# Turning x and C on TensorE, emptying PSUM in pairs, and a reordered head in a fused state-space and feed-forward kernel

## The chip, the core and the metric

The kernel runs on one core of a Trainium2 chip. A core has TensorE (PE: matrix products into PSUM, eight banks of 512 fp32 columns), VectorE (DVE), ScalarE (ACT), GpSimd (POOL) and the queue of SyncE (SP); DMAs are issued from SP, ACT or POOL. The metric is the device time of one execution in microseconds (us).

## What is computed

x is 2048 tokens by 448 features. A gate mixes a diagonal complex state-space model (448 states) with a feed-forward block (width 1792):

```python
g = sigmoid((x * gate_w).sum(-1, keepdims=True))
dt = exp(log_dt); Lam = Lambda_re + 1j * Lambda_im
Lam_bar = exp(dt * Lam)
Bu = einsum("bld,pd->blp", x, ((Lam_bar - 1) / Lam)[:, None] * Bmat)
h[t] = Lam_bar * h[t - 1] + Bu[:, t, :]          # over 2048 steps
a = 2.0 * einsum("blp,dp->bld", h, Cmat).real + x * Dskip
b = silu(x @ w1) @ w2
out = g * a + (1 - g) * b
```

All inputs and the output are bf16.

## The kernel before

**Tiling.** Tokens go in four chunks of 512 (`tc`), features and states in blocks of 128; 448 = 3 x 128 + 64. The real and imaginary parts of the 448 states fill seven slots of 128 lanes (0 to 3 real, 4 to 6 imaginary; slot 3 holds the last 64 of both). The recurrence is made real: tables COS and SIN rotate the input B x of each chunk, a real scan (`tensor_tensor_scan`, one per slot and chunk, decay `rc`) runs over it into `Gf`, and the result is rotated back into `H`.

**Stages.** `x_products` (L586 to L617) computes tiles of x times w1 (F, 14 per chunk) and of x times B (B, 7 per chunk). Two tiles run side by side, each on 64 rows of TensorE at a time; a pair takes two halves, of 4 and 3 steps, and the first half of the next pair is issued before the second of the present one. `evict` (L575) empties each tile by ScalarE: F with Silu into `aT`, B into `U`. `lanes` (L628) does the rotation, scans and back rotation of a chunk on VectorE; each scanned slot goes from fp32 `Gf` to bf16 `Gb` by a DMA of the GpSimd queue (L659). `gates` (L731) computes g. `ffn2` (L682) is the product with w2 for 128 tokens, emptied by ScalarE into `fe` and added to `xnat` by an accumulating DMA. `readout` (L701) is the product of H with the scaled C (`CP`), emptied by VectorE (L710) into `ot` and stored. `readout_weights` (L716) makes CP from C and the scales `sc1`, `nsc1`, `sc2`.

**Transposed inputs.** TensorE needs x with features on partitions. Chunk 0 is turned on TensorE (`x0_transposes`, L437); chunks 1 to 3 and both parts of C come by transposing DMAs on SP (`loadT`, L361 to L363). B is turned on TensorE (`b_transposes`, L549). The three parameter rows reach all lanes by a small product with the identity (L469); ScalarE takes their Exp; four phase tables are made on VectorE (L495 to L502) and turned into SIN and COS by ScalarE; GpSimd copies them to slots 4 to 6 (L505, L506) and computes the scales in some 25 four-column operations (L512 to L544).

**What sets the order.** Every operation is registered with an estimated cost and a priority. A list scheduler (`Plan.order`, L97) simulates the engines and writes one fixed order for each; TensorE keeps the order of the program, the others take the earliest ready operation, the lower priority number first. PSUM banks are handed out in that simulation. On the chip each engine works through its list in order and waits by semaphores.

The order of the loads on SP (L366 to L412) is: x of chunk 0, w1 columns 0 to 512 in two cuts, B, w1 columns 512 to 1792 in two cuts, x of chunk 1 transposed, gate_w and Dskip spread over the partitions (`gwb`, `dkb`), w2, then x of chunks 1 to 3 plain and of 2 and 3 transposed, then C transposed.

The order of stages on TensorE is written out at the end of the function (L750 to L785):

```python
x_products(F(0, 0, 4)); b_transposes(...)      # slots 0,1 / 2 / 4,5 / 6 / 3
x_products(B(0) + F(0, 4, 5)); lanes(0); gates(0)
x_products(F(0, 5) + B(1)); lanes(1); gates(1)
readout_weights(); ffn2(0..3)
x_products(F(1) + F(2, 0, 1) + B(2)); lanes(2); gates(2)
ffn2(4..7); readout(0..3)
x_products(F(2, 1) + B(3)); lanes(3); gates(3)
readout(4..7); ffn2(8..11)
x_products(F(3))
readout(8..11); ffn2(12..15); readout(12..15)
```

Of the kernel before, what the change touches and what calls it, by code (L numbers as in the profile page):

```python
# [32 lines left out]
class Ps:  # L33


    __slots__ = ("bank", "users", "left")

    def __init__(self):
        self.bank = None
        self.users = 0  # L40
        self.left = 0
# [7 lines left out]
class Plan:  # L49
# [4 lines left out]
    INORDER = ("pe",)  # L54

# [41 lines left out]
    def order(self):  # L97
# [8 lines left out]
        free = {}  # L106
# [5 lines left out]
        def earliest(o):  # L112
            t = 0.0
            for d in o.deps:
                p = ops[d]
                t = max(t, p.end + (self.HOP[p.eng] if p.eng != o.eng else 0.02))
            new = [x for x in o.ps_w if x.bank is None]
            if new:
                open_ = sorted(banks[b] for b in range(8) if holder[b] is None)
                if len(open_) < len(new):  # L120
                    return None
                t = max(t, open_[len(new) - 1] + 0.1)
            return t

        while len(done) < len(ops):
# [22 lines left out]
            if o.sem is not None:  # L148
                slow = o.eng == "pool"
                free[o.eng] = t + (1.0 if slow else 0.45)  # L150
                pipe[o.eng] = max(pipe.get(o.eng, 0.0), t + 0.9) + o.bytes / (100e3 if slow else 260e3)
                o.end = pipe[o.eng] + 0.7
            else:
                free[o.eng] = o.end = t + o.cost
# [4 lines left out]
            for tk in o.ps_w:  # L159
                if tk.bank is None:  # L160
                    b = min((x for x in range(8) if holder[x] is None), key=lambda x: (banks[x], x))
                    tk.bank = b
                    tk.left = tk.users
                    holder[b] = tk
            for tk in o.ps_r:
                tk.left -= 1
                banks[tk.bank] = max(banks[tk.bank], o.end)
                if tk.left == 0:
                    holder[tk.bank] = None
# [10 lines left out]
class Waits:  # L180
# [14 lines left out]
    def put(self, o):  # L195
        eng = o.eng
        reads = o.reads + [f"bank{t.bank}" for t in o.ps_r]
        writes = o.writes + [f"bank{t.bank}" for t in o.ps_w]
# [54 lines left out]
def bass_gated_mix__ssm_conv_s5__dense_activation_silu__prompt_kernel(nc, A_x, A_Lambda_re, A_Lambda_im, A_B_re, A_B_im, A_C_re, A_C_im,  # L253
               A_log_dt, A_Dskip, B_x, B_w1, B_w2, gate_w, out):
    with ExitStack() as ctx:
# [12 lines left out]
        BT = sb("BT", [128, 4, NSLOT * 128], BF16)  # L268
        CTr = sb("CTr", [128, 4, D_MOD], BF16)
        CTi = sb("CTi", [128, 4, D_MOD], BF16)  # L270
# [7 lines left out]
        H = [sb(f"H{k}", [128, NSLOT, CH], BF16) for k in range(4)]  # L278
# [8 lines left out]
        ct = [sb(f"ct{k}", [128, D_MOD], F32) for k in range(2)]  # L287
# [11 lines left out]
        prm = sb("prm", [3, 512], BF16)  # L299
        pc = sb("pc", [128, 3, 4], F32)  # L300
# [29 lines left out]
        def bk(t):  # L330
            return ps[:, t.bank, :]
# [24 lines left out]
        def load(q, dst, src, name, nbytes, prio=None, after=()):  # L356
            nl[0] += 1
            prio = nl[0] if prio is None else prio
            P.add(q, lambda e: e.dma_start(dst, src), list(after), name.split(), 0.3, prio, sem(), nbytes, tag="ld " + name)  # L359

        def loadT(dst, src, name, nbytes, after=()):  # L361
            nl[0] += 1
            P.add("sp", lambda e: e.dma_start_transpose(dst, src), list(after), [name], 0.3, nl[0], sem(), nbytes, tag="ldT " + name)  # L363


        for k, v in enumerate((A_Lambda_re, A_Lambda_im, A_log_dt)):  # L366
            load("act", prm[k:k + 1, 64:512], v.rearrange("(o n) -> o n", o=1), f"prm{k}", 896, k)
# [3 lines left out]

        def load_w1(c0, c1, name):
            load("sp", w1s[:, 0:3, c0:c1], B_w1[0:384, c0:c1].rearrange("(b p) f -> p b f", p=128), name + "a", 768 * (c1 - c0))
            load("sp", w1s[:, 3, c0:c1], B_w1[320:448, c0:c1], name + "b", 256 * (c1 - c0))

        w1cuts = [0, 256, 512, 1152, 1792]
        load_w1(0, 256, "w1_0")
        load_w1(256, 512, "w1_1")
        Bnat = H[3][:, :, 0:D_MOD]
        load("sp", Bnat[:, 0:3, :], A_B_re[64:448, :].rearrange("(b p) d -> p b d", p=128), "H3_0 H3_1 H3_2", 384 * 896)  # L380
        load("sp", Bnat[:, 4:7, :], A_B_im[64:448, :].rearrange("(b p) d -> p b d", p=128), "H3_4 H3_5 H3_6", 384 * 896)
        load("sp", Bnat[0:64, 3, :], A_B_re[0:64, :], "H3_3", 64 * 896)
        load("sp", Bnat[64:128, 3, :], A_B_im[0:64, :], "H3_3i", 64 * 896)
        btn = {s: [f"BT{s}"] for s in range(7)}
        load_w1(512, 1152, "w1_2")
        load_w1(1152, 1792, "w1_3")

        def load_xT(tc):
            for c, n in ((0, 3), (3, 1)):
                loadT(xT[:, c:c + n, tc * CH:(tc + 1) * CH],  # L390
                      x2[tc * CH:(tc + 1) * CH, XCOL[c]:XCOL[c] + 128 * n], f"xT{tc}{c}", CH * 256 * n)

        def load_xn(tc):
# [3 lines left out]
        load_xT(1)  # L397
        load("sp", gwb[:, :],
             gate_w.rearrange("(o n) -> o n", o=1).partition_broadcast(128).rearrange("p o n -> p (o n)"),
             "gwb", 128 * 896)  # L400
        load("sp", dkb[:, :],
             A_Dskip.rearrange("(o n) -> o n", o=1).partition_broadcast(128).rearrange("p o n -> p (o n)"),
             "dkb", 128 * 896)
# [417 lines left out]
```

## Time and profile before

| | us |
|---|---|
| median of 3 runs | 150.91 (150.79 to 153.16) |
| the profiled execution | 151.09 |
| its span, first to last instruction | 149.3 |
| TensorE busy | 137.2 |
| VectorE busy | 120.7 |
| ScalarE busy | 87.1 |
| GpSimd busy | 65.7 |

The page lists busy times, the span in 40 slices, DMA queues, the chain of waits that ended last, groups of instructions and DMA issues. A group line reads: line, engine, operation, output<-inputs, shapes, xcount | busy us, mean ns of one | idle time before them on their engine and what ended it. L603 is the product of `x_products`, L688 that of `ffn2`, L707 that of `readout`, L557 the transposes of B, L626 every two-input elementwise operation of VectorE. Matmuls are pipelined, so the mean of one is longer than their distance.

### The profile page before, as it was taken

Reading aid. Unit: us, or ns where it says so; the run is one execution under the profiler, and the core shown is the slowest. Engines: PE = TensorE matmul, PEld = TensorE weight load, DVE = VectorE, ACT = ScalarE, POOL = GpSimd, SP = SyncE. Lnnn points to the kernel's source line nnn. Section 1 sums busy time; section 2 is a strip of 40 time slices with the busy share of each in tenths; the row PEclk is TensorE's granted clock in tenths of the full one; section 3 lists DMA queues with packets and bytes.
Section 4 is the critical chain, followed back from the end, with each engine's and each line's share of the span. In section 5 each row is a group of like instructions: output and inputs, shape, how many; then the busy total and the mean of one; then the engine's idle time right before and its main releaser. Section 6 shows DMA issues by size and latency. Waiting matters only on the chain.

```text
span 149.3 us, 2605 instructions
## 1 busy us (share of the span) xinstructions
PE 137.2 (92%) x979; PEld 65.4 (44%) x979; DVE 120.7 (81%) x154; ACT 87.1 (58%) x179; POOL 65.7 (44%) x108
## 2 busy tenths in 40 slices
PE   6897925999999999999999999999999999999592
PEld 2563402344454444445554444455554445555250
DVE  0589399999199996299998999989999994946742
ACT  3579808397888498888999588720312773031100
POOL 7130796079296949245385000422750241175200
PEclk9999995699999999999999999999999999999999
DMA  4999999999999002236659100175572245547322
GB/s 135 254 296 282 60 289 317 149 258 209 212 141 164 22 0 33 31 68 102 107 79 176 39 0 0 35 141 127 93 111 31 31 75 101 129 66 101 47 56 82
DMA packets 26962, 17.35 MB, mean 116 GB/s; under 512 B 11587, under 2 KB 26822, under 8 KB 26950
## 3 DMA queue, kind: packets, MB, share of 16 engines
q1 hardware_dynamic: 19712, 10.64, 32.2%
q0 software_dynamic: 7232, 6.56, 28.8%
q8 instruction: 7, 0.11, 0.3%
q14 instruction: 5, 0.04, 0.1%
q10 hardware_dynamic: 6, 0.00, 0.0%
HBM read 6.31 MB, written 1.84 MB: 55 GB/s over the span
## 4 chain that ended last, share of the span: by engine, by line
PE 74%; SPq 8%; DVE 7%; DMA 5%; issue 2%; ACT 1%; POOL 1%; DVEq 0%; POOLq 0%
PE ps L603 38%; PE ps L688 21%; PE ps L707 14%; SPq L359 5%; SPq L363 4%; DMA gwb<-in_gate_w_dram 3%; DVE H L626 2%; DMA Gb<-Gf 2%; DVE xg L626 2%; DVE Gf L502 1%; DVE ot L710 1%; DVE PO L626 1%; DVE Gf L656 1%; ACT COS L503 0%; POOL xnat L696 0%
## 5 line engine op out<-in xcount | busy, mean ns | idle before, releaser
L603 PE MATMUL ps<-xT,w1s 64*128 64x512 bf16 x392 | 49.4, 391 | 5.0 <-ACT U L581 4.4
L688 PE MATMUL ps<-w2s,aT 128*128 128x448 bf16 x224 | 43.0, 353 | 0.0
L578 ACT ACTIVATE aT<-ps 128x512 bf16<-128x512 f32 x56 | 30.5, 598 | 15.7 <-PE ps L603 15.7
L603 PEld LDWEIGHTS ps<-xT,w1s 64*128 64x128 bf16 x392 | 20.7, 97 | 30.5 <-ACT U L581 4.9
L688 PEld LDWEIGHTS ps<-w2s,aT 128*128 128x128 bf16 x224 | 21.8, 98 | 20.9 <-issue 0.8
L359 POOL DMA_DIRECT2D Gb<-Gf x36 | 20.5, 620 | 20.9 <-DVE Gf L656 20.7
L603 PE MATMUL ps<-xT,BT 64*128 64x512 bf16 x196 | 25.3, 376 | 0.9 <-DVE BT L564 0.9
L656 DVE TENSOR_TENSOR_SCAN Gf<-rc,gin,H 128x512 f32<-128x512 f32 x21 | 25.8, 1268 | 0.1
L694 ACT ACTIVATE fe<-ps,g 128x448 bf16<-128x448 f32 x16 | 10.0, 630 | 23.9 <-PE ps L688 17.2
L707 PE MATMUL ps<-CP,H 128*128 128x448 bf16 x112 | 21.9, 353 | 1.9 <-DVE H L626 1.9
L696 POOL DMA_DIRECT2D xnat<-fe x16 | 14.9, 942 | 16.8 <-ACT fe L694 16.7
L710 DVE SCALAR_TENSOR_TENSOR ot<-ps,g,xnat 128x448 bf16<-128x448 f32 x16 | 10.9, 678 | 7.0 <-PE ps L707 6.4
L707 PEld LDWEIGHTS ps<-CP,H 128*128 128x128 bf16 x112 | 10.7, 98 | 12.8 <-DVE H L626 2.3
L581 ACT ACTIVATE U<-ps 128x512 bf16<-128x512 f32 x28 | 15.1, 599 | 2.1 <-PE ps L603 2.1
L603 PEld LDWEIGHTS ps<-xT,BT 64*128 64x128 bf16 x196 | 10.7, 94 | 12.4 <-DVE BT L564 1.1
L359 POOL DMA_DIRECT2D U<-U x8 | 4.8, 604 | 16.0 <-ACT U L581 16.0
L626 DVE TENSOR_TENSOR H<-Gb,COS 128x3584 bf16<-128x3584 bf16 x4 | 8.1, 2018 | 3.2 <-DMA Gb<-Gf 3.2
L626 DVE TENSOR_TENSOR xg<-xnat,gwb 128x1792 bf16<-128x1792 bf16 x4 | 5.9, 1477 | 5.8 <-ACT junk L740 3.3
L740 ACT ACTIVATE junk<-xg 128x448 bf16<-128x448 bf16 x16 | 9.2, 575 | 2.2 <-DVE xg L626 2.0
L747 ACT ACTIVATE xnat<-xnat,g 128x448 bf16<-128x448 bf16 x16 | 10.1, 662 | 0.1
L626 DVE TENSOR_TENSOR PI<-U,SIN 128x512 bf16<-128x512 bf16 (+2 forms) x13 | 9.0, 724 | 0.1
L626 DVE TENSOR_TENSOR H<-H,PI 128x512 bf16<-128x512 bf16 (+1 forms) x10 | 8.7, 896 | 0.1
(89 smaller groups left out, 119.7 us busy)
## 6 DMA issues: line engine op xcount, KB each, us to landing
Gb<-Gf POOLq DMA_DIRECT2D x28, 128.0 KB, 2.4
xnat<-fe POOLq DMA_DIRECT2D x16, 112.0 KB, 2.6
out_dram<-ot SPq DMA_DIRECT2D x16, 112.0 KB, 1.7
w2s<-in_B_w_dram SPq DMA_DIRECT2D x1, 1568.0 KB, 11.1
xnat<-in_A_x_dram SPq DMA_DIRECT2D x3, 448.0 KB, 5.0
w1s<-in_B_w_dram SPq DMA_DIRECT2D x2, 480.0 KB, 5.9
U<-U POOLq DMA_DIRECT2D x8, 64.0 KB, 1.9
Gb<-Gf POOLq DMA_DIRECT2D x8, 64.0 KB, 3.2
```

Of the source, the lines that this page charges most:

```text
L359: P.add(q, lambda e: e.dma_start(dst, src), list(after), name.split(), 0.3, prio, sem(), nbytes, tag="ld " + name)
L578: ACT(lambda e: e.activation(aT[tc % 2][:, k, :], bk(tk), AF.Silu), [tk, "tbl"], [f"aT{tc % 2}_{k}"], act_cost(512), 5, "silu")
L581: ACT(lambda e: e.activation(U[:, k, :], bk(tk), AF.Copy), [tk], [f"U{k}"], act_cost(512), 5, "U")
L603: r = pe.matmul(bk(tk), w[p0:p0 + 64, i, c:c + 128], xT[p0:p0 + 64, i, tc * CH:(tc + 1) * CH], start=(h == 0 and n == 0), stop=(h == 1 and ...
L626: DVE(lambda e: e.tensor_tensor(o, a, b, op), r, w, dve_cost(n, 2), prio, tag)
L656: DVE(lambda e, s=s, b=b, init=init: e.tensor_tensor_scan(Gf[:, s, :], rc[:, b:b + 1].to_broadcast([128, CH]), A[:, s, :], init, ALU.mult, ...
L688: r = pe.matmul(bk(tk)[:, 0:D_MOD], aT[tc % 2][:, fb, o:o + 128], w2s[:, fb, :], start=(fb == 0), stop=(fb == NFB - 1))
L694: ACT(lambda e: e.activation(f[:, :], bk(tk)[:, 0:D_MOD], AF.Copy, scale=g1[:, tb:tb + 1]), [tk, f"g1_{tc}"], [fn], act_cost(448, 1), 7, "fe")
L696: P.add("pool", lambda e: e.dma_start(Tb[:, tb, :], f[:, :], accum_op=ALU.add), [fn, f"Tb{tb}"], [f"Tb{tb}"], 0.3, 2, sem(), 115000, tag=" ...
L707: r = pe.matmul(bk(tk)[:, 0:D_MOD], H[tc][:, s, o:o + 128], CP[:, s, :], start=(s == 0), stop=(s == NSLOT - 1))
L710: DVE(lambda e: e.scalar_tensor_tensor(ot[tb % 3][:, :], bk(tk)[:, 0:D_MOD], g[:, tb:tb + 1], Tb[:, tb, :], ALU.mult, ALU.add), [tk, f"g_{ ...
L747: ACT(lambda e, tb=tb: e.activation(Tb[:, tb, :], xnat[:, tb, :], AF.Copy, scale=g[:, tb:tb + 1]), [f"xd{tc}", f"g_{tc}"], [f"Tb{tb}"], ac ...
```

## The change

Six edits, made together:

- No transposing DMA is left. x of chunks 1 to 3 is loaded once, plain, and turned by 16 TensorE transposes a chunk into two neighbouring PSUM banks, emptied in one operation (VectorE for chunk 1, ScalarE for 2 and 3). C is loaded plain into a part of H2's memory (in four DMAs), turned per slot into one PSUM bank and scaled straight from there; slots 3 of both parts are one.
- A pair of `x_products` takes two neighbouring banks, and where both tiles are of one kind they are emptied by one operation of 1024 columns. B of chunk 0 is emptied by VectorE.
- The loads are reordered: w1 in three cuts (0, 512, 768, 1792), gwb and dkb ahead of the last cut, x of chunk 1 and w2 behind it, then C, then x of chunks 2 and 3.
- The parameter product stands ahead of the x transposes; Exp becomes a power of e on GpSimd, so one ScalarE table load goes; five warm-up matmuls in place of seven; the last phase table has a buffer of its own; the copies of SIN and COS to slots 4 to 6 go from GpSimd to VectorE.
- The last chunk's Gb comes from ScalarE copies in place of DMAs.
- The stage order is changed, and the planner's costs for DMAs, evictions and scans, and its handing out of banks, which now knows pairs.

```diff
-        w1cuts = [0, 256, 512, 1152, 1792]
+        w1cuts = [0, 512, 768, 1792]
...
-        load_xT(1)
...
+        for dst, src, name in ((gwb, gate_w, "gwb"), (dkb, A_Dskip, "dkb")):
+            load("sp", dst[:, :], ...)
+        load_w1("sp", w1cuts[2], w1cuts[3], 0, "w1_2")
+        load_w1("sp", w1cuts[2], w1cuts[3], 1, "w1_2")
...
+        load_xn(1)
         load("sp", w2s[:, :, :], B_w2.rearrange("(fb p) d -> p fb d", p=128), "w2", F_FF * 896)
-        load_xn(1)
-        load_xT(2)
+        load_C()
         load_xn(2)
-        load_xT(3)
         load_xn(3)
-        for dst, src, name in ((CTr, A_C_re, "Cr"), (CTi, A_C_im, "Ci")):
-            loadT(dst[:, 0:3, :], src[:, 64:448], name + "a", 448 * 768)
-            loadT(dst[:, 3:4, :], src[:, 0:128], name + "b", 448 * 256)
...
-            for _ in range(7):
+            for _ in range(5):
                 r = pe.matmul(bk(tkz), zt[:, 0:128], zt, start=True, stop=True)
...
+        POOL(lambda e: e.tensor_tensor(dtc[:, :], eul[:, :], LDT, ALU.pow), ["pc", "eul"], ["dtc"], 0.35, 0)
...
+        def x_transposes(tc, who):
+            tk = Ps(2)
+            def mm(pe):
+                for q in range(4):
+                    for b in range(4):
+                        o = (q % 2 * 4 + b) * 128
+                        r = pe.transpose(bk(tk, q // 2).bitcast(BF16)[:, o:o + 128],
+                                         xnat[:, 4 * tc + b, XCOL[q]:XCOL[q] + 128], ident[:, :])
+                return r
+            PE(mm, [f"xn{tc}", "ident"], [tk], 16 * 0.056, f"xT{tc}")
...
+            if who == "dve":
+                DVE(lambda e: e.tensor_copy(dst, src()), [tk], [f"xT{tc}"], 1.25, 4, "xTe")
+            else:
+                ACT(lambda e: e.activation(dst, src(), AF.Copy), [tk], [f"xT{tc}"], act_cost(2048), 4, "xTe")
...
-        POOL(lambda e: e.tensor_copy(COS[:, 4:7, :], COS[:, 0:3, :]), ...)
-        POOL(lambda e: e.tensor_single_scalar(SIN[:, 4:7, :], SIN[:, 0:3, :], -1.0, ALU.mult), ...)
+        DVE(lambda e: e.tensor_copy(COS[:, 4:7, :], COS[:, 0:3, :]), ...)
+        DVE(lambda e: e.tensor_single_scalar(SIN[:, 4:7, :], SIN[:, 0:3, :], -1.0, ALU.mult), ...)
...
+        def evict(pair, tk):
+            kinds = [t[0] for t in pair]
+            for k, n in ((0, 2),) if kinds[0] == kinds[-1] and len(pair) == 2 else ((0, 1), (1, 1))[:len(pair)]:
...
+                if tc == 0:
+                    DVE(lambda e, src=src, dst=dst: e.tensor_copy(dst, src()), [tk], [f"U{m}" for m in names], 0.15 + 0.53 * n, 5, "U")
...
+                    if tc + 1 < NCH:
+                        load("pool", dst, src, name, 180000, 1, [f"Gf{s}"])
+                    else:
+                        ACT(lambda e, dst=dst, src=src: e.activation(dst, src, AF.Copy), [f"Gf{s}"], [name], 0.56, 6, "Gb")
...
+        def readout_weights(k):
+            tk = Ps()
...
+                        r = pe.transpose(bk16(tk)[:, o:o + 112], Cnat[:, b, c0:c0 + 128], ident[0:112, 0:112])
...
+            ACT(lambda e: e.activation(c[:, 0, :], im(), AF.Copy, scale=sc2[:, k:k + 1]), [tk, "sc2"], ...)
...
+            DVE(lambda e: e.scalar_tensor_tensor(CP[:, k, :], re(), sc1[:, k:k + 1], c[:, 0, :], ALU.mult, ALU.add), ...)
...
         x_products(F(0, 0, 4))
         b_transposes([0, 1], "dve")
-        b_transposes([2], "act")
-        b_transposes([4, 5], "dve")
-        b_transposes([6], "act")
+        b_transposes([4, 5], "act")
+        b_transposes([2], "dve")
+        b_transposes([6], "dve")
         b_transposes([3], "dve")
-        x_products(B(0) + F(0, 4, 5))
+        x_products(F(0, 4, 6) + B(0) + F(0, 6, 7))
         lanes(0)
+        x_products(F(0, 7) + B(1), {1: xt(1, "dve")})
         gates(0)
-        x_products(F(0, 5) + B(1))
         lanes(1)
         gates(1)
-        readout_weights()
-        for tb in range(0, 4):
-            ffn2(tb)
+        for f in G(0) + cp(0) + G(1) + xt(2, "act") + cp(1) + G(2) + cp(2) + G(3) + cp(3):
+            f()
         x_products(F(1) + F(2, 0, 1) + B(2))
...
-        for tb in range(4, 8):
-            ffn2(tb)
-        for tb in range(0, 4):
-            readout(tb)
+        for f in G(4) + xt(3, "act") + G(5, 6, 7) + C(0, 1, 2, 3):
+            f()
```

`G`, `C`, `cp` and `xt` stand for `ffn2`, `readout`, `readout_weights` and `x_transposes`. `{1: xt(1, "dve")}` puts chunk 1's transposes between the first half of the third pair and the second half of the second; the fourth pair's first half is the first to read them.

More of the change, by code (lines that the diff above doesn't have):

```diff
@@ L105, in order @@
                 ready.setdefault(o.eng, []).append(o)
-        free = {}
+        free = {e: 0.72 for e in ("pe", "act", "dve", "pool", "sp")}
         pipe = {}
@@ L148, in order @@
             if o.sem is not None:
[L149 to L152, printed above, removed]
+                free[o.eng] = t + o.cost
+                q = "pool" if o.eng == "pool" else "hw"
+                pipe[q] = max(pipe.get(q, 0.0), t + 0.9) + o.bytes / self.RATE[q]
+                o.end = pipe[q] + 0.8
             else:
@@ L196, in put @@
         eng = o.eng
-        reads = o.reads + [f"bank{t.bank}" for t in o.ps_r]
-        writes = o.writes + [f"bank{t.bank}" for t in o.ps_w]
+        reads = o.reads + [f"bank{t.bank + k}" for t in o.ps_r for k in range(t.n)]
+        writes = o.writes + [f"bank{t.bank + k}" for t in o.ps_w for k in range(t.n)]
         need = {}
```

292 lines of the change are left out of this document (160 added, 132 removed).

## The prediction

> **What bounds the kernel now.** I read the busy times first, then the chain of waits (its totals, then its pieces in order of time), then windows of one microsecond over the start, then the groups by form, then single engines in order of time.
>
> ```profile
> span 149.3 us, 2605 instructions
> PE 137.2 (92%) x979; PEld 65.4 (44%) x979; DVE 120.7 (81%) x154; ACT 87.1 (58%) x179; POOL 65.7 (44%) x108
> PEclk9999995699999999999999999999999999999999
> GB/s 135 254 296 282 60 289 317 149 258 209 212 141 164 22 0 33 31 68 102 107 79 176 39 0 0 35 141 127 93 111 31 31 75 101 129 66 101 47 56 82
> PE 74%; SPq 8%; DVE 7%; DMA 5%; issue 2%; ACT 1%; POOL 1%; DVEq 0%; POOLq 0%
> ```
>
> TensorE is busy 92% of the span and carries 74% of the chain, so what it does and waits for sets the time. VectorE, at 81%, stands close behind. Two slices of the clock row, from about 22 to 30 us, are at half.
>
> ```profile
> 8.26 3.94 SPq L363
> 12.25 1.34 SPq L363
> 13.63 4.66 DMA gwb<-in_gate_w_dram
> 18.41 2.65 DVE xg L626
> 21.06 1.64 DVE Gf L502
> 22.73 0.72 ACT COS L503
> 23.45 0.49 ACT U L581
> 23.99 13.79 PE ps L603 x97
> 37.78 10.70 PE ps L688 x56
> 48.48 16.73 PE ps L603 x154
> 140.96 5.48 PE ps L707 x28
> ```
>
> The columns are start, length, what. The two transposing loads of x hold SP's queue for 5.3 us (3.94 + 1.34), gwb is issued only behind them and lands at 18.3; VectorE stands in order before xg, then does the last phase table, then ScalarE its cosine, and only then the U evictions that free PSUM for TensorE at 23.99.
>
> ```profile
> 25.00:26.00 1.00, 1.00 (x8) 0.30 (x4) 1.00 (x3) 0.88 (x2) 0.02 (x1) 0.50 1.95 233
> 29.00:30.00 1.00, 1.00 (x12) 0.46 (x10) 0.87 (x4) 0.38 (x1) 0.00 (x0) 1.00 1.30 193
> L603 PE MATMUL ps<-xT,w1s 64*128 64x512 bf16 x392 | 49.4, 391 | 5.0 <-ACT U L581 4.4 <-ACT dtc L475 0.6
> L603 PE MATMUL ps<-xT,BT 64*128 64x512 bf16 x196 | 25.3, 376 | 0.9 <-DVE BT L564 0.9
> L707 PE MATMUL ps<-CP,H 128*128 128x448 bf16 x112 | 21.9, 353 | 1.9 <-DVE H L626 1.9
> ```
>
> Each window row ends in the granted clock, the DMA share and GB/s: half clock at 25, full again at 29. The groups give all of TensorE's large waits from the first product on: 4.4, 0.9 and 1.9 us. The half clock has its own price: 154 matmuls took 16.73 us later (0.1086 each), so the 97 from 23.99 should have taken 10.54 and took 13.79, a loss of 3.25. From 24 us to the end TensorE has only the last wait, so 4.4 + 3.25 + 0.9 + 1.9 = 10.45 us is all that can be won there.
>
> **The change, part by part.** First the new TensorE work.
>
> ```profile
> L557 PE MATMUL ps<-ident,H 128*128 128x128 bf16 x28 | 1.7, 219 | 0.3 <-DMA H<-in_A_B_im_dram 0.3
> 9.88 1.72 PE L557 MATMUL ps<-ident,H 128*128 128x128 bf16 x28 [0.30 <-DMA H<-in_A_B_im_dram]
> L469 PE MATMUL ps<-ident,prm 3*128 3x3 bf16 x4 | 0.2, 163 | 0.0
> L564 DVE COPY BT<-ps 128x1024 bf16<-128x1024 bf16 x2 | 1.4, 688 | 0.7 <-PE ps L557 0.7
> L564 DVE COPY BT<-ps 128x512 bf16<-128x512 bf16 x1 | 0.4, 417 | 0.0
> ```
>
> Turning x (chunks 1 to 3) takes 3 x 16 transposes, C 4 x 8: 80. At 1.72 / 28 = 0.061 us they cost 4.9 us, all on TensorE and thus on the path. The parameter product now stands ahead of the x transposes: 0.25 us.
>
> Chunk 1's transposes stand one half (3 steps of two concurrent matmuls, 6 x 0.1086 = 0.65 us) before the half that reads them, and VectorE must empty 2048 columns in between. From 1024 in 0.688 and 512 in 0.417 that copy is 1.23 us. So TensorE waits at least 1.23 - 0.65 = 0.6, and up to 0.75 more if VectorE is inside another operation; I take 1.0. The copies of chunks 2 and 3 go to ScalarE with most of an ffn2 stage (10.70 us) between, at nothing; were that cover gone they would cost at most four times the 598 ns of a 512-column row below, 2.4 us each. C's plain loads now go ahead of the last two chunks of x on SP, whose readers are two stages away: nothing.
>
> The B transposes' wait (0.9) goes: products of F blocks 4 and 5 now stand before the first B product. They need w1's second cut, the last of 2.05 MB (x 0.46, w1 0.52, B 0.80, w1 0.26); by the GB/s row, in slices of 3.73 us, that has passed by 0.50 + 0.95 MB at 7.5 us and 0.60 / 296 GB/s = 2.0 more, 9.5, and TensorE wants it when the B transposes end, now 11.6. The last cut of w1 goes behind gwb and dkb, two more issues of SP's half microsecond; TensorE wants it some six us later. Fewer warm-up matmuls and the Exp that became a power on GpSimd (no row shows it; GpSimd's four-column operations run from 0.19 to 1.99 us) lie ahead of the phase tables, behind which TensorE has transposes of B and six F blocks to do: nothing, and up to 2 us of VectorE if the power is slow.
>
> VectorE gets the U evictions of chunk 0, the chunk-1 copy and two table copies from GpSimd:
>
> ```profile
> 16.86 4.12 POOL L506 TENSOR_SCALAR SIN<-SIN 128x1536 bf16<-128x1536 bf16 x1
> L710 DVE SCALAR_TENSOR_TENSOR ot<-ps,g,xnat 128x448 bf16<-128x448 f32 x16 | 10.9, 678 | 7.0 <-PE ps L707 6.4 <-issue 0.5
> L626 DVE TENSOR_TENSOR PO<-Gb,SIN 128x1536 bf16<-128x1536 bf16 x4 | 3.8, 950 | 0.1
> L626 DVE TENSOR_TENSOR xg<-xnat,gwb 128x1792 bf16<-128x1792 bf16 x4 | 5.9, 1477 | 5.8 <-ACT junk L740 3.3 <-DMA gwb<-in_gate_w_dram 2.5
> ```
>
> By 0.678 us for 448 columns from PSUM, a pair (1024) lies between that and 1.55; I take 1.2, so 3 pairs and a single are 4.3 us. The table copies are at most 0.95 each. With 1.2 that is 7.4 us more. Against it: the wait for gwb (2.5) goes, since only those 2.05 MB are ahead of gwb; and xg, which took 2.65 beside GpSimd's 4.12 us table copy, should take the mean of the other three, (5.9 - 2.65) / 3 = 1.08, a gain of 1.6. One CP operation fewer is 0.7. VectorE thus carries some 2.6 us net more in the head, but starts its first lanes sooner and has later idle time to use:
>
> ```profile
> 40.59 1.09 DVE L626 TENSOR_TENSOR xg<-xnat,gwb 128x1792 bf16<-128x1792 bf16 x1 [3.13 <-ACT junk L740]
> 63.34 0.68 DVE L719 SCALAR_TENSOR_TENSOR CP<-CTr,sc,ct 128x448 bf16<-128x448 bf16 x1 [2.75 <-ACT ct L718]
> 129.20 2.45 DVE L656 TENSOR_TENSOR_SCAN Gf<-rc,gin,H 128x512 f32<-128x512 f32 x2
> 135.68 2.03 DVE L626 TENSOR_TENSOR H<-Gb,COS 128x3584 bf16<-128x3584 bf16 x1 [3.19 <-DMA Gb<-Gf]
> L578 ACT ACTIVATE aT<-ps 128x512 bf16<-128x512 f32 x56 | 30.5, 598 | 15.7 <-PE ps L603 15.7
> ```
>
> In the tail the last chunk's Gb goes over ScalarE (about 0.6 us a slot by the 598 ns row, on an engine then nearly idle) and no longer over DMA: the 3.19 us wait goes. Before, the last readout could start at 140.96; now at about 137.8 without any gain upstream. TensorE wants it at 139.1 (140.96 less 1.9) minus its net gain so far, 4.4 + 3.25 + 0.9 - 4.9 - 0.25 - 1.0 = 2.4, so 136.7. VectorE has to find 1.1 us in 3.13 + 2.75 of earlier idle time; I expect most, leaving 0.3. The planner's new costs reshuffle every queue, which no row prices: from 1.3 us won (both my new waits, 1.0 and 0.3, gone) to the rivals below.
>
> Emptying pairs in one ScalarE operation saves at most 0.6 us of every 1.2, but ScalarE waits 15.7 us for TensorE in this group: nothing, at the price that a bank is held some 0.5 longer, covered by three other pairs of banks.
>
> The sum: 10.45 won, less 4.9, 0.25, 1.0 and 0.3, is 4.0. Span 149.3 - 4.0 = 145.3. The profiled execution took 151.09, 1.79 beyond its span, and is 0.18 over the median, 150.91. So 147.1 us, 2.5% under the median. With no new wait at all: 145.8; and counting the last transpose's own 219 ns out of the 1.72, (1.72 - 0.22) / 27 = 0.056 each, 0.5 less: 145.3.
>
> **The rivals.** *VectorE becomes the bound.* If its 2.6 us more are not recovered and the last scan ends that much later, the last readout starts between 137.8 and 140.4; 5.48 us of TensorE and the 2.9 that follow it now (149.3 - 146.44) give spans of 146.2 to 148.8, so 148.0 to 150.6; with a slow power up to 2 more. I take 149.8. For it: 81% of the span, and 2.6 us more. Against: the 5.9 us of idle.
>
> *GpSimd's scales come late; slower.*
>
> ```profile
> 59.60 0.21 POOL L520 TENSOR_TENSOR sc<-cw 128x4 f32<-128x4 f32 x1
> 1.18 3.17 PE L431 MATMUL ps<-PO 128*128 128x512 bf16 x7 [1.18 <-DVE PO L415]
> 6.38 3.20 PE L603 MATMUL ps<-xT,w1s 64*128 64x512 bf16 x28 [0.59 <-ACT dtc L475]
> ```
>
> C now lies transposed in four PSUM banks until ScalarE and VectorE have scaled it, and that wants sc, which GpSimd finishes at 59.8 today. TensorE would start ffn2 at 37.78 - 8.55 + 0.98 + 0.25 + 1.0 = 31.5, put C there from 34, and reach the next products at 31.5 + 10.7 + 48 x 0.061 = 45. ScalarE takes its work in order, so behind a waiting scale the silus wait, banks run out two pairs later, about 48, and every microsecond beyond that is lost; with a wait of 4.4 or more the 3.25 of half clock come on top. At 53 us that is 5 + 3.25: 155. For it: today's 59.8. Against: the 4.12 us table copy and a shorter one leave GpSimd, and today nothing pressed sc to be early.
>
> *The clock comes up late.* The seven warm-up matmuls run 0.45 us apiece, twice the 0.229 of a step of the first products (3.20 / 14). With five and then a gap until the parameters land, the first 28 may run at half: up to 3.2 us more, 150.3. [...]
>
> *The transposes were not what held the loads.*
>
> ```profile
> xT<-in_A_x_dram SPq DMA_TRANSPOSE x6, 5.6
> xnat<-in_A_x_dram SPq DMA_DIRECT2D x3, 448.0 KB, 5.0
> ```
>
> A chunk of x lands in 5.6 us transposed and 5.0 plain. If bytes alone make the head late, its 4.4 and 3.25 stay: 154.8. [...] Landing times agree; the 3.94 and 1.34 us of SP's queue do not.
>
> **How the numbers follow.** Forecast 0.60 (147.1; nearly all of it over 2% faster, some 0.05 within), VectorE 0.14 (149.8), clock 0.08 (150.3), GpSimd's scales 0.15 (155), loads 0.03 (154.8). 2%, about what a measurement of this kernel can tell, is 3.0 us: below 147.9 is faster, above 153.9 slower. Faster 0.56 (0.55 and a little of the VectorE case), within 0.26, slower 0.18. The range reaches from 145.2 to 151.7, the upper parts of the VectorE and clock cases; outside lie the scales, the loads and 0.02 below.
>
> **What would show it.** Right: no TensorE wait over 2 us after the first product, a clock row without a half after the first slices, ffn2 starting near 31.5 us instead of 37.78, 128-column matmuls up by some 80 with 4.9 us or less, a wait near 1 us behind the xT copy of chunk 1. Wrong: ScalarE waiting for sc or the silus' banks holding TensorE near 48 us; a last readout that waits over 1 us for H; a half clock under the first 28 products.

## The result and the profile after

| | before | after |
|---|---|---|
| median of 4 runs, us | 150.85 (150.78 to 153.16) | 148.82 (148.56 to 149.57) |
| the profiled execution, us | 151.09 | 149.57 |
| its span, us | 149.3 | 147.6 |

The ratio is 0.987, with a 95% interval of 0.984 to 0.990: 1.3% faster, within the 2% called no change. Medians, here and below, are over all executions of a kernel; ratios and their intervals leave out executions more than 1.5% above its fastest. The profile's page after, busy times, clock row and chain totals:

```profile
span 147.6 us, 2710 instructions
PE 141.3 (96%) x1057; PEld 69.8 (47%) x1057; DVE 122.8 (83%) x160; ACT 88.2 (60%) x143; POOL 52.1 (35%) x102
PEclk9999999999999999999999999999999999999999
PE 94%; DVE 3%; issue 1%; ACT 0%; DVEq 0%
```

TensorE went from 74% of the chain to 94%, and the half slices of the clock row are gone. Most of what it waited for before is no longer there; what is left is nearly all its own work, and that has grown by 4.1 us. The chain of waits after, in order of time (start, length, what):

```profile
6.89 5.69 PE ps L642 x28
12.58 0.57 PE ps L585 x8
...
14.65 10.96 PE ps L642 x100
25.62 1.01 PE ps L508 x16
26.63 0.02 issue
26.66 1.23 DVE xT L515
27.89 0.05 issue
27.93 6.87 PE ps L642 x62
34.80 2.75 PE ps L732 x14
37.55 0.40 PE ps L768 x8
...
40.60 0.89 PE ps L508 x16
...
67.46 0.89 PE ps L508 x16
...
139.48 5.31 PE ps L751 x28
```

L642 is now the product of `x_products`, L732 that of `ffn2`, L751 that of `readout`; L508 are the transposes of x, L768 those of C (four groups of 0.40). From 14.65 on the only break is the copy L515 of chunk 1's transposes, for which TensorE waits 0.56 us. The first ffn2 starts at 34.80 instead of 37.78, 3 us earlier. Behind it come 3.4 us of transposes of x and C, and at the end the wait of 1.9 us for the last H is gone; the last product ends at 144.79 instead of 146.44, 1.65 us earlier.

The first line is what the forecast did not have: 28 matmuls in 5.69 us, where the kernel before took 3.20. Windows of one microsecond, first after, then before (the window, its length, PE's busy share and its matmuls, the other engines, and at the end the granted clock, DMA share and GB/s):

```profile
8.00:9.00 1.00, 1.00 (x7) 0.36 (x5) 1.00 (x3) 0.07 (x1) 0.87 (x2) 1.00 0.95 224
```

```profile
8.00:9.00 1.00, 1.00 (x14) 0.48 (x11) 1.00 (x3) 0.21 (x1) 0.63 (x2) 1.00 0.93 317
```

Seven matmuls against fourteen in the same microsecond, both fully busy: exactly half pace. The clock column says 1.00 in both, so it does not show this; it has to be read from the matmuls.

**The ledger.** Two terms of the forecast can now be measured better. Products of chunk 0 and B of chunk 1 between the B transposes and the first ffn2 are 168 matmuls; a later run (load order and table copies, below) does them without a break in 18.46 us. Before, they ran from 12.54 to 37.78, so 25.24 - 4.37 (the wait) - 18.46 = 2.4 us was the price of the half clock, not 3.25. The chain of before counts 97 matmuls from 23.99 on, but 64 of the 168 had run ahead of the wait, so 104 were left; the run with the table copies alone, below, shows 104 at the same place. Against the 4.0 us of the forecast, then: first matmuls -2.5, half clock -0.85, first product 0.51 later instead of 0.25, 0.4 of the wait for B's transposes still there; on the other side 80 transposes for 1.01 + 0.89 + 0.89 + 4 x 0.40 = 4.4 instead of 4.9, the wait for L515 0.56 instead of 1.0, the last readout's 0.3 not needed, and a 0.3 us wait for B's load gone. That makes 1.55, beside the 1.65 measured.

### The profile page after: what moved, and what is told of

Its sections match the earlier page's. It is cut to its first block, busy times and chain, and to the rows that moved or that the text cites. A ratio compares the mean times of both kernels' runs of the same rounds, so it can differ in the third digit from the quotient of the medians.

```text
span 147.6 us, 2710 instructions
## 1 busy us (share of the span) xinstructions
PE 141.3 (96%) x1057; PEld 69.8 (47%) x1057; DVE 122.8 (83%) x160; ACT 88.2 (60%) x143; POOL 52.1 (35%) x102
## 3 DMA queue, kind: packets, MB, share of 16 engines
HBM read 7.17 MB, written 1.84 MB: 61 GB/s over the span
## 4 chain that ended last, share of the span: by engine, by line
PE 94%; DVE 3%; issue 1%; ACT 0%; DVEq 0%
PE ps L642 45%; PE ps L732 29%; PE ps L751 15%; PE ps L508 2%; PE ps L444 2%; PE ps L484 1%; PE ps L768 1%; DVE BT L592 1%; DVE xT L515 1%; DVE ot L754 0%; ACT xT L493 0%; PE ps L585 0%; DVE PO L427 0%; PE ps L455 0%; DVE prm L457 0%
## 5 line engine op out<-in xcount | busy, mean ns | idle before, releaser
L642 PE MATMUL ps<-xT,w1s 64*128 64x512 bf16 x392 | 50.0, 391 | 1.7 <-ACT xT L493 0.8
L732 PE MATMUL ps<-w2s,aT 128*128 128x448 bf16 x224 | 43.7, 353 | 0.0
L614 ACT ACTIVATE aT<-ps 128x1024 bf16<-128x1024 f32 (+1 forms) x30 | 28.8, 964 | 17.7 <-PE ps L642 17.6
L642 PEld LDWEIGHTS ps<-xT,w1s 64*128 64x128 bf16 x392 | 20.7, 97 | 26.9 <-issue 3.8
L732 PEld LDWEIGHTS ps<-w2s,aT 128*128 128x128 bf16 x224 | 21.6, 98 | 20.2 <-issue 0.4
L642 PE MATMUL ps<-xT,BT 64*128 64x512 bf16 x196 | 25.5, 376 | 0.0
L738 ACT ACTIVATE fe<-ps,g 128x448 bf16<-128x448 f32 x16 | 10.2, 639 | 23.9 <-PE ps L732 23.3
L380 POOL DMA_DIRECT2D Gb<-Gf x27 | 16.8, 653 | 8.1 <-DVE Gf L696 8.1
L696 DVE TENSOR_TENSOR_SCAN Gf<-rc,gin,H 128x512 f32<-128x512 f32 x14 | 16.9, 1264 | 0.1
L751 PE MATMUL ps<-CP,H 128*128 128x448 bf16 x84 | 16.4, 353 | 0.0
L642 PEld LDWEIGHTS ps<-xT,BT 64*128 64x128 bf16 x196 | 10.7, 94 | 11.5
L751 PEld LDWEIGHTS ps<-CP,H 128*128 128x128 bf16 x84 | 8.1, 98 | 7.9 <-issue 0.4
L621 ACT ACTIVATE U<-ps 128x1024 bf16<-128x1024 f32 (+1 forms) x12 | 10.5, 913 | 0.9 <-PE ps L642 0.9
L380 POOL DMA_DIRECT2D U<-U x8 | 4.7, 589 | 17.7 <-ACT U L621 15.9
L666 DVE TENSOR_TENSOR PO<-Gb,SIN 128x1536 bf16<-128x1536 bf16 (+1 forms) x8 | 8.6, 1088 | 0.8 <-issue 0.5
L696 DVE TENSOR_TENSOR_SCAN Gf<-rc,gin,H2C 128x512 f32<-128x512 f32 x7 | 8.6, 1268 | 0.0
L696 DVE TENSOR_TENSOR_SCAN Gf<-rc,H 128x512 f32<-128x512 f32 x7 | 8.3, 1208 | 0.0
```

What stands on the lines that cost most here:

```text
L614: ACT(lambda e, src=src, dst=dst: e.activation(dst, src(), AF.Silu), [tk, "tbl"], [f"aT{tc % 2}_{m}" for m in names], act_cost(512 * n), 5 ...
L621: ACT(lambda e, src=src, dst=dst: e.activation(dst, src(), AF.Copy), [tk], [f"U{m}" for m in names], act_cost(512 * n), 5, "U")
L642: r = pe.matmul(bk(toks[k], b), weights(tile, p0, p0 + 64, i), xT[p0:p0 + 64, i, tc * CH:(tc + 1) * CH], start=(h == 0 and n == 0), stop=( ...
L666: DVE(lambda e: e.tensor_tensor(o, a, b, op), r, w, dve_cost(n, 2), prio, tag)
L696: DVE(lambda e, s=s, b=b, init=init: e.tensor_tensor_scan(Gf[:, s, :], rc[:, b:b + 1].to_broadcast([128, CH]), A[:, s, :], init, ALU.mult, ...
L732: r = pe.matmul(bk(tk)[:, 0:D_MOD], aT[tc % 2][:, fb, o:o + 128], w2s[:, fb, :], start=(fb == 0), stop=(fb == NFB - 1))
```

## The experiments

Each kernel ran beside the kernel before on the same chip; ratios are to that, with 95% intervals.

**Is the slow start a matter of the warm-up?** The changed kernel with seven warm-up matmuls again:

```diff
-            for _ in range(5):
+            for _ in range(7):
```

> The changed kernel with seven warm-up matmuls again instead of five, nothing else; the planner's cost for them is left, so every queue keeps its order. Theory A (the first products ran at half clock because the warm-up is shorter and a gap follows it): the first 28 matmuls take 3.2 us again instead of 5.69, the rest keeps its place behind them, and the time falls by 2 to 2.5 us, to about 146.5. Rival B (the first products were slow for another reason: they wait for w1, or the clock comes up when it likes): the 28 still take over 5 us, the time stays near 148.8.

Median 148.59 us, 0.985 (0.976 to 0.995), its runs spread from 147.75 up; the profiled one took 147.77. TensorE's matmuls in order of time there, the first 14 of the 28:

```profile
4.92 0.23 PE L455 MATMUL ps<-ident,prm 3*128 3x3 bf16 x4 [0.58 <-DVE prm L457]
5.09 1.07 PE L484 MATMUL ps<-ident,xnat 128*128 128x128 bf16 x16
7.54 1.69 PE L642 MATMUL ps<-xT,w1s 64*128 64x512 bf16 x14 [1.38 <-DVE xT L491]
```

In that execution the clock was up (28 in 3.19 us); everything in front came 0.65 us later, and ffn2 started 1.84 us earlier, at 32.96. That is the 1.8 us by which this profiled run beats the other one. But not every run followed: two took 147.8, the others 149.4 and 150.3, and no trace shows how those two began.

The reverse, five warm-ups in the kernel before:

```diff
-            for _ in range(7):
+            for _ in range(5):
```

> The kernel before with five warm-up matmuls instead of seven, nothing else. Theory A: its first 28 matmuls take 5 to 6 us instead of 3.20; but the wait of 4.4 us that follows at 19.6 us is ended by VectorE and ScalarE, not by TensorE, so most of the loss is taken back there and the time grows by under 1 us. Rival B: the 28 stay at 3.2 us. Rival C (the loss is simply added, since the head is a chain through TensorE): 2.5 us slower, 153.4.

151.56 us, 1.003 (0.998 to 1.007). The slow start is there, and its cost does not show in the times. The profile's TensorE lines

```profile
6.17 2.32 PE L603 MATMUL ps<-xT,w1s 64*128 64x512 bf16 x10 [0.54 <-ACT xT L453]
...
25.38 3.17 PE L603 MATMUL ps<-xT,w1s 64*128 64x512 bf16 x14 [4.37 <-ACT U L581]
```

show the same 4.37 us wait as before: TensorE came later to a wait that ended later too (gwb landed at 19.3 in place of 18.3). The wait ends with the U evictions behind gwb, whenever TensorE gets there. So while gwb bounded the head, a slow start could hide in that wait; the change took this cover away.

All profiled executions together, time of the first 28 products:

| warm-ups | us, one execution each |
|---|---|
| 7 | 3.20 (before), 3.19, 5.07, 3.20, 3.20, 4.92, 3.20 |
| 5 | 5.69 (after), 5.16, 4.57, 4.69, 4.87, 4.64, 5.75 |

With seven, five executions of seven start at full pace; with five, none. Seven executions of each are few, but the warm-up is all that separates the first two experiments from their kernels. (The list takes in the profiles of the runs that follow; in the one with fillers, two more matmuls stand behind the seven.)

**What held the head: the transposing DMAs, or the order of the loads?** The kernel before, its six transposing loads of x and four of C untouched, with gate_w and Dskip loaded ahead of the second half of w1:

```diff
+        load("sp", gwb[:, :], ...)
+        load("sp", dkb[:, :], ...)
         load_w1(512, 1152, "w1_2")
...
         load_xT(1)
-        load("sp", gwb[:, :], ...)
-        load("sp", dkb[:, :], ...)
```

> The kernel before with only the loads of gwb and dkb moved ahead of w1's third cut and so ahead of the transposing loads of x; every transpose stays a DMA, TensorE's order stays. Theory D (what held TensorE at 19.6 us was gwb behind the transposing loads on SP): the wait of 4.4 us and the half clock after it (3.25 us) go or shrink to under 1 us, the first ffn2 starts near 31 instead of 37.8 us, and the time falls to 145 to 148, limited at the end by the wait for the last H. Rival E (gwb was only the last of several late things: phase tables, GpSimd's table copies, x turned by DMA): a wait of 2 us or more stays at that place and the time stays over 149.

147.02 us, 0.977 (0.970 to 0.984): this one edit brings more than the whole change. The 4.4 us wait and the half clock are gone, and ffn2 starts at 32.84, though this profiled execution had a slow start (5.07). Something new stands in VectorE's row, and GpSimd's row has its two table copies at the same time:

```profile
20.39 6.29 DVE L626 TENSOR_TENSOR H<-U,COS 128x1024 bf16<-128x1024 bf16 x1 [0.23 <-ACT U L581]
...
27.95 0.68 DVE L626 TENSOR_TENSOR H<-U,COS 128x1024 bf16<-128x1024 bf16 x1
```

```profile
21.39 1.50 POOL L505 COPY COS<-COS 128x1536 bf16<-128x1536 bf16 x1
22.84 4.13 POOL L506 TENSOR_SCALAR SIN<-SIN 128x1536 bf16<-128x1536 bf16 x1
```

An operation of 0.68 us took 6.29 and ended at 26.68, about when GpSimd was through with its two table copies (22.84 + 4.13 = 26.97). VectorE has 20% of that chain, and TensorE waited 2.2 us near 50 us and 1.8 for the last H. The operation is long only beside the copies: of the same form, the one at 27.95 takes 0.68, and with the copies on VectorE (below) this one takes 0.66. By what the copies lengthen it is not shown. Spans on GpSimd are rough: by these rows the operation began 1.0 us ahead of the first copy.

**Load order and table copies in one.** To the edit above, the two table copies on VectorE as the change has them, and the change's tail (the last chunk's Gb by ScalarE, slot 3 scanned first):

```diff
-        POOL(lambda e: e.tensor_copy(COS[:, 4:7, :], COS[:, 0:3, :]), ...)
-        POOL(lambda e: e.tensor_single_scalar(SIN[:, 4:7, :], SIN[:, 0:3, :], -1.0, ALU.mult), ...)
+        DVE(lambda e: e.tensor_copy(COS[:, 4:7, :], COS[:, 0:3, :]), ...)
+        DVE(lambda e: e.tensor_single_scalar(SIN[:, 4:7, :], SIN[:, 0:3, :], -1.0, ALU.mult), ...)
...
-            for s in (0, 4, 1, 5, 2, 6, 3):
+            for s in (3, 0, 4, 1, 5, 2, 6) if tc else (0, 4, 1, 5, 2, 6, 3):
...
+                    if tc + 1 < NCH:
+                        load("pool", dst, src, name, 180000, 1, [f"Gf{s}"])
+                    else:
+                        ACT(lambda e, dst=dst, src=src: e.activation(dst, src, AF.Copy), [f"Gf{s}"], [name], 0.56, 6, "Gb")
```

> The kernel before with three of the change's edits alone: gwb and dkb ahead of w1's third cut, the copies of SIN and COS on VectorE instead of GpSimd, the last chunk's Gb by ScalarE instead of DMA. All transposes of x and C stay DMAs, every tile is emptied by itself. Theory D with H (the head's wait came from the load order and GpSimd's copies, and each transpose on TensorE is pure cost): no TensorE wait over 1 us after the first product, no half clock after 10 us, the end 1.8 us (last H) and 2.2 us (wait at 49.8) ahead of the run with gwb alone, 143 to 145, and some 4 us faster than the changed kernel. Rival K (the changed kernel's other parts, its pairs and its plain loads, are needed to keep TensorE fed): waits of together over 3 us appear, and the time is 147 or more.

143.24 us, 0.947 (0.942 to 0.952). The same without the tail, Gb by DMA again:

> The kernel before with gwb and dkb early and the copies of SIN and COS on VectorE, the last Gb by DMA as before: between the run with gwb alone (147.0) and the one with all three edits (143.2). Theory T (GpSimd's table copies had held a VectorE operation of 0.68 us for 6.29, and the wait of TensorE at 49.8 came of it): no VectorE operation near 20 us beyond 1.3 us, the wait of 2.2 us is gone, and the last readout still waits for H, by 3 to 4 us now that TensorE is earlier: 145 to 146. Rival U (the tail edit is worth nothing and the tables all): 143.2 to 143.7, the last readout without a wait.

142.87 us, 0.945 (0.940 to 0.951): the tail edit was worth nothing, and a loss for leaving it out did not come. Together with the one before it, within each other's intervals, this is the fastest kernel of the study, with two edits to the kernel before. Its chain in order of time, and the VectorE operation that had taken 6.29:

```profile
6.78 4.92 PE ps L603 x28
...
14.31 18.46 PE ps L603 x168
32.77 10.70 PE ps L688 x56
43.47 16.73 PE ps L603 x154
...
134.08 5.31 PE ps L707 x28
```

```profile
20.87 0.66 DVE L626 TENSOR_TENSOR H<-U,COS 128x1024 bf16<-128x1024 bf16 x1
```

From 14.31 to the end TensorE is never kept waiting: 168, 56, 154 matmuls follow each other. All transposes of x and C are DMAs here. This profiled execution started slowly and took 144.34; its other runs lie between 142.32 and 142.92.

The changed kernel holds both of these edits and is some 6 us slower. The two profiled executions, both with a slow start, show where: its first ffn2 starts 2.0 us later (34.80 against 32.77) and its last product ends 5.4 us later. Of that, 4.4 us are the 80 transposes and 0.56 the wait for L515. So the rest of the change cost about what it added to TensorE.

The table copies alone, with the loads in their old order:

> The kernel before with only the copies of SIN and COS on VectorE instead of GpSimd; the loads keep their order. Theory V (the load order and GpSimd's copies lengthen the same chain: gwb lands at 18.3, then xg takes 2.65 and the last phase table 1.71 beside GpSimd instead of 1.08 and 0.42): the chain after gwb shortens by 1.6 + 1.3 = 2.9 us, TensorE's wait of 4.4 us falls to under 2, the clock does not halve behind it, and the time falls by 3 to 6 us, to 145 to 148. Rival W (gwb's landing is what counts): the wait stays above 3 us, the clock halves, at most 1.5 us faster, over 149.

146.88 us, 0.974 (0.968 to 0.980). Three views of its profile: VectorE in order of time, the chain, and a window.

```profile
20.00 1.09 DVE L626 TENSOR_TENSOR xg<-xnat,gwb 128x1792 bf16<-128x1792 bf16 x1 [3.38 <-DMA gwb<-in_gate_w_dram]
21.01 0.42 DVE L502 TENSOR_SCALAR Gf<-Gf 128x512 int32<-128x512 int32 x1
```

```profile
8.31 3.78 SPq L363
12.14 1.34 SPq L363
13.52 6.36 DMA gwb<-in_gate_w_dram
...
22.72 13.09 PE ps L603 x104
```

```profile
24.00:25.00 1.00, 1.00 (x8) 0.38 (x6) 1.00 (x4) 0.61 (x2) 0.00 (x0) 0.50 1.08 368
```

gwb is as late as ever (19.9), but xg takes 1.09 and the last phase operation 0.42, where before they took 2.65 and 1.64 beside GpSimd's two copies. From the start of xg to TensorE's next product it is 2.72 us (20.00 to 22.72), before 5.58 (18.41 to 23.99): 2.9 shorter, as expected. TensorE's wait fell by only 2.0, to 2.42, mainly because gwb landed 1.6 us later in this execution. So the wait had two causes in a row, the late gwb and the slow operations behind it. They do not split it: the load order alone took all of it away, the copies alone 2.0 us in this execution. The expectation that the clock would hold through so short a wait was wrong: it halved, and 104 matmuls took 13.09 instead of 104 x 0.1086 = 11.3.

**The start again.** To the kernel with load order, table copies and tail, two filler matmuls directly ahead of the first product, which close the gap in TensorE's work there:

```diff
+        def warm2(pe):
+            for _ in range(2):
+                r = pe.matmul(bk(tkz2), zt[:, 0:128], zt, start=True, stop=True)
+            return r
...
+        PE(warm2, ["PO0"], [tkz2], 0.0, "warm2")
```

> The kernel before with gwb early, the table copies on VectorE and the last Gb by ScalarE, and two more warm-up matmuls behind the parameter product, in the gap in which TensorE waits for the x transposes to be emptied. Theory R (the clock comes up only after a stretch in which TensorE is busy without a gap, and when that stretch ends is chance; full activity until the first product makes it certain): the first 28 matmuls take 3.2 to 4 us in every execution, the times lie within 0.7 us of each other, at 143, and none is near 146. Rival S (it is chance, whatever fills the gap): again some executions 1.5 to 3 us over the others. Cost if useless: up to 0.4 us.

Median 143.72 us, 0.950 (0.944 to 0.955), where the kernel without them had 143.24 and 0.947: no gain. The profiled execution began at full pace (3.20), but the times lie between 142.65 and 149.45, and the expected spread of 0.7 us did not come. No trace shows how the late ones began, so whether more activity in front makes the onset surer is not shown. Why TensorE is at full pace by 4 to 7 us in one execution and only at 10 to 12 in another stays open.

**What the rest of the change does.** Turning chunks 2 and 3 of x by DMA again, in the changed kernel, behind all other loads:

```diff
         load_xn(3)
+        for tc in (2, 3):
+            for c, n in ((0, 3), (3, 1)):
+                P.add("sp", lambda e, tc=tc, c=c, n=n: e.dma_start_transpose(...), ...)
...
-        for f in G(0) + cp(0) + G(1) + xt(2, "act") + cp(1) + G(2) + cp(2) + G(3) + cp(3):
+        for f in G(0) + cp(0) + G(1) + cp(1) + G(2) + cp(2) + G(3) + cp(3):
...
-        for f in G(4) + xt(3, "act") + G(5, 6, 7) + C(0, 1, 2, 3):
+        for f in G(4) + G(5, 6, 7) + C(0, 1, 2, 3):
```

> The changed kernel with chunks 2 and 3 of x turned by transposing DMAs on SP again, issued behind all other loads; chunk 1 and C stay on TensorE. Theory H (turning on TensorE costs its own length, since TensorE has no gap to hide it, and the DMAs were hidden there): the two groups of 16 transposes (0.89 us each) go and the time falls by 1.8 us, to about 147. Rival I (VectorE's end comes next): the last H, ready 3.5 us before TensorE wants it in the changed kernel, moves with the new order and takes back a part; less than 1 us faster. Rival J (the transposing DMAs land late or slow others): not faster, a TensorE wait ahead of chunk 2's or 3's products.

147.51 us, 0.976 (0.969 to 0.984). Its 32 transposes (0.89 + 0.89 us) are gone and no wait takes their place: in the profile the first ffn2 starts at 34.82, as in the changed kernel, and the gain lies behind it. The kernel of the next paragraph, measured on the same chip and as slow as the changed one, took 149.22: a gain of 1.7, about the transposes' own time. On TensorE they are pure cost here, and by DMA, where no critical load stands behind them, free.

The last chunk's Gb by DMA again:

```diff
-                    if tc + 1 < NCH:
+                    if True:
```

> The changed kernel with the last chunk's Gb by DMA of the GpSimd queue again, as in the kernel before. Theory L (VectorE has 3.5 us to spare at the end of the changed kernel): the last H comes about 3.2 us later, at 139, still before TensorE wants it at 139.4, and the time stays within 0.5 us of 148.8. Rival M (the copies on ScalarE are what took the last wait away): a wait of 1 us or more before the last readout and as much more time.

149.22 us, 0.987 (0.981 to 0.994): no difference to the changed kernel, and no wait ahead of the last readout.

Chunk 1's transposes one pair earlier:

```diff
-        x_products(F(0, 7) + B(1), {1: xt(1, "dve")})
+        x_products(F(0, 7) + B(1), {0: xt(1, "dve")})
```

> The changed kernel with the transposes of chunk 1 one pair earlier, so that a whole pair of products lies between them and the half that reads them. Theory F (TensorE waits there only for VectorE's copy): the wait of 0.6 us goes and the time falls by 0.5 us, with the first 28 matmuls as slow as in the changed kernel. Rival G (VectorE is late anyway, and the copy only moves the wait elsewhere): no difference.

148.91 us, 0.988 (0.982 to 0.995). In its chain the transposes are followed by products at once:

```profile
23.17 1.00 PE ps L508 x16
24.17 8.96 PE ps L642 x82
```

so the 0.56 us wait is gone, but the medians, 148.91 and 148.82, do not show it: the scatter of the start is larger.

Emptying the two tiles of a pair by two operations, each planned by itself:

```diff
-            for k, n in ((0, 2),) if kinds[0] == kinds[-1] and len(pair) == 2 else ((0, 1), (1, 1))[:len(pair)]:
+            for k, n in ((0, 1), (1, 1))[:len(pair)]:
```

> The changed kernel with every tile of a pair emptied by its own operation again, the two neighbouring banks kept. Theory N (ScalarE waits for TensorE, so fewer and longer operations save nothing on the path): ScalarE's busy time rises by about 5 us, TensorE gets no new wait, the time stays within 0.5 us of 148.8. Rival O (the pair operation is what keeps VectorE and ScalarE ahead of TensorE in the head): a TensorE wait of over 1 us in the first 35 us and a time over 150.

155.12 us, 1.027 (1.019 to 1.034), some 6 us slower than the changed kernel. Its chain, the list of TensorE's waits (total, times, longest) and the clock row:

```profile
40.67 1.09 DVE xnat L666
41.76 5.01 DVE Gf L696 x5
...
51.23 0.60 DVE CP L782
51.84 0.05 issue
51.88 18.82 PE ps L642 x146
```

```profile
PE ps L642 <- DVE CP L782: 3.8, 1, 3.8
```

```profile
PEclk9999999999999659999999999999999999999999
```

The planner's simulation, given other operations and costs, wrote other orders. On VectorE five scans stand ahead of the operations L779 and L782 that scale C out of PSUM. On GpSimd the issues of the DMAs behind those scans stand ahead of the last scale, `sc2`, which is ready at 47.34 in place of 40.73; ScalarE's part of the scaling, which needs it, starts at 47.37. C's transposes kept their banks, TensorE stood 3.8 us from 48 on, and the clock halved: 146 matmuls took 18.82 instead of 146 x 0.1086 = 15.9. Is that the eviction or the order? The same two operations inside one planned operation, so that the planner writes the same lists:

```diff
-                    ACT(lambda e, src=src, dst=dst: e.activation(dst, src(), AF.Silu),
+                    ACT(lambda e, src=src, dst=dst, n=n: [e.activation(dst[:, m, :], src()[:, m, :], AF.Silu) for m in range(n)][-1],
```

> The changed kernel with every tile of a pair emptied by its own instruction, but the two instructions kept as one operation of the planner, so that no queue changes its order (in the run that split them in the plan, the scaling of C came behind five scans on VectorE, TensorE stood without PSUM for 3.8 us and the clock halved). Theory P (that run was slow by the order, not by the eviction): ScalarE's busy time rises by 1 to 5 us, the scaling of C keeps its place, TensorE has no wait over 1 us after 15 us, the time is within 0.7 us of 148.8. Rival Q (single evictions hold the banks too long): waits appear ahead of 50 us and the time is over 151.

149.40 us, 0.991 (0.987 to 0.994). ScalarE is busy 1.6 us longer (89.8 against 88.2) and TensorE has no wait over 0.8 us behind the warm-up. The median is 0.6 us above that of the changed kernel, and the two intervals overlap; so emptying in pairs is worth little, if anything, and nearly all of the 6 us were the order.

## Why the prediction was right and where it was not

- **The number.** The time lies in the stated range of 145.2 to 151.7, but the forecast itself, 147.1 and over 2% faster, did not come: 1.3% is the outcome that had 0.26. (147.1 is the sum for a profiled execution, span 145.3 + 1.79, and belongs beside 149.57; for the median it would have been 146.9.) The ledger shows errors of 4.0 us one way (2.5 + 0.85 + 0.4 + 0.26) and 1.55 the other. That they partly cancel is luck.
- **The head.** Right: the 4.4 us wait, its half clock and most of the 0.9 went, and behind the first product no TensorE wait of over 1 us is left. But ffn2 starts at 34.80, not near the 31.5 that was named. The cause of the wait was told only in part. SP's queue and the order of the loads were named; of GpSimd's copies, the 1.6 us on xg were seen, but neither the same on the operation behind it (1.64 for 0.42) nor that moving the copies alone would bring 2.6%. The half clock's 3.25 was too large, because the 97 matmuls of the chain line were 104.
- **"Fewer warm-up matmuls ... nothing".** This step failed. It reckoned with the phase tables, which indeed had cover, and left the first 28 products to a rival with 0.08. That rival came true beside the forecast, with 2.5 of the 3.2 us that it gave at most. That 147.1 + 2.5 gives the profiled run's 149.57 is chance: the other errors, 1.5 us each way, cancel. The five later profiles of the changed kernel's family with five warm-ups started slowly as well; so did the kernel before with five.
- **The transposes.** 4.4 instead of 4.9, all on the path as said; the wait behind chunk 1's was 0.56 instead of 1.0.
- **VectorE as the bound.** It did not happen. The last H in VectorE's lines of the changed kernel,

```profile
133.83 2.03 DVE L666 TENSOR_TENSOR H<-H,PO 128x3584 bf16<-128x3584 bf16 x1
```

  ends at 135.86, 3.6 us before TensorE starts the last readout (139.48). The 1.9 us wait went entirely, though not through ScalarE's Gb: with DMAs it went too.
- **GpSimd's scales.** GpSimd's line for the last scale in the changed kernel, and ScalarE's first operation that needs it,

```profile
39.29 1.44 POOL L547 TENSOR_TENSOR sc<-cw 128x4 f32<-128x4 f32 x1
```

```profile
40.77 0.63 ACT L774 ACTIVATE ct<-ps,sc 128x448 f32<-128x448 bf16 x1 [1.08 <-POOL sc L547]
```

  show it ready at 40.7, 19 us earlier than before. ScalarE waited 1.08 us for it, one of the signs that the prediction named, but TensorE was not held. The danger was real all the same: the kernel with single evictions stood at that place, near 48 us, with a wait and a half clock, at 155.12 us, the 155 of this rival. There `sc2` came at 47.34 and VectorE's scans were in the way as well. Both orders had changed, and no run separates them.
- **Loads.** Bytes alone did not make the head late; but neither were transposing DMAs the trouble as such: with gwb ahead of them, all ten do no harm. Plain loads can hold SP's queue as long: the first load of C held it 5.07 us in the changed kernel, with nothing urgent behind it.

## What to carry to other kernels

When a wait bounds the head, find which transfer it is for and try moving that one load first: here that and two copies taken off GpSimd gave 5.5%, where the whole change, which holds both, gave 1.3%. On a kernel whose bound is TensorE, work moved onto TensorE costs its own time, as the 4.4 us of transposes did here; a wait that is removed also uncovers what it hid, here a slow start. With a planner that writes the order from costs, hold the order fixed when one operation is to be judged: the same edit cost 0.6 us, within the noise, or 6.

## What the runs showed of the hardware

- TensorE begins at half pace in all 14 profiled executions: a warm-up matmul of 512 columns takes 0.45 to 0.46 us (3.17 / 7, 2.31 / 5), where one of 448 columns in ffn2 takes 0.19 later (10.70 / 56). In some executions this lasts until 4 to 7 us, an estimate from the rows: there the first 28 products take 3.20 us, and the 16 transposes of x ahead of them 1.07 to 1.91, where 16 take 0.89 later. In others it lasts until 10 to 12 us, also an estimate (by twice the excess over 3.20: 6.89 + 2 x 2.49 = 11.9 in the changed kernel). In the windows of one microsecond from 1 to 14 us the profile's granted clock shows 1.00, in the changed kernel as in the one before.
- Once up, the clock stood waits of 1.9 us (before) and 2.2 (gwb early) and halved with waits of 2.42 (table copies alone), 3.8 (single evictions) and 4.37 (before). In the kernel before it fell near 22.1 (0.53 in the window from 22 to 23), 2.4 us after TensorE stopped at 19.62; with the table copies alone near 23.3 (0.63 in the window from 23 to 24), 3.0 us after TensorE stopped at 20.30 and 0.5 after it began again. What decides on the moment is not shown.
- The half clock lasted 3.4 us with the table copies alone and twice that in the kernel before, by windows of one microsecond (0.63 from 23, 0.50, 0.50, 0.66 from 26; and 0.53 from 22, five at 0.50, 0.56 from 28). In the executions of the kernel before that ran beside the experiments the mean clock falls into two groups as well, 0.986 to 0.989 with times of 150.0 to 150.9 us and 0.974 to 0.977 with 150.7 and more. The profiled one, at 0.977, is of the second group, so the 2.4 us of the ledger are the price of the longer half clock.
- Beside GpSimd's two copies a VectorE operation with two inputs (L626, 1024 columns) took 6.29 us instead of 0.68 (gwb early), another (xg) 2.65 instead of 1.09, and one with a single input (L502) 1.64 instead of 0.42 (both before, against table copies alone).
